# Eight full expert tiles ahead of the last routing, a hand-made TensorE order, and logits with moving tokens: attention and a routed expert layer on one core

## The chip, the cores and the metric

The kernel runs on one core of a Trainium2 chip. The metric is the device time of one execution in microseconds (us); lower is better. A core has TensorE (matmul), VectorE, ScalarE, GpSimd (POOL in the profile), SyncE (SP, here the engine that issues the large transfers) and 16 DMA engines that all queues share. All data are float32, apart from the masks.

## The reference

Attention with a window of 32 (heads 0 to 3: the last 32 positions; heads 4 to 7: every fourth of the last 128), then a layer of eight experts with one expert to a token. A token takes the expert with the largest logit, unless its local gate is at least 0.5: then it keeps the expert of the token before it.

```python
# q, k, v: (8, 8, 576, 64); x: (8, 576, 512); w_gate (512, 8); w1 (8, 512, 1024); w2 (8, 1024, 512)
scores = np.where(masks, scale * q @ k.T, -1e9)
x = softmax(scores) @ v                         # heads side by side: 512 features
logits = einsum('bsd,de->bse', x, w_gate)
local_gate = sigmoid(x @ w_local)
for b in range(B):
    prev_e = -1
    for s in range(S):
        fresh_e = argmax(logits[b, s])
        e = fresh_e if s == 0 or local_gate[b, s] < 0.5 else prev_e
        prev_e = e
        p = softmax(logits[b, s])
        h = np.maximum(x[b, s] @ w1[e], 0.0)
        out[b, s] = p[e] * (h @ w2[e])
```

## The kernel before, in words

Two stages follow each other. The attention stage loops over 32 pairs of heads, four pairs (NP = 4) to a batch. `load(n)` puts three transfers for pair n on SP's queue (`kt`, `qt`, `vt`; 1.27 MB together, three buffers each). `scores(n)` makes twelve matmul instructions into three PSUM tiles `sc` (six products; a float32 product is two instructions); VectorE adds the mask (line 232) and ScalarE takes the exponential (235). `values(n)` multiplies by `vt` into `pv` (278), and VectorE divides by the row sums (280 to 282) into `x`.

After the four pairs of a batch comes its routing, which the dictionary `steps` spreads over the following iterations. `store` writes `x` to `xd` in DRAM. `x_turn` transposes `x` into `xt` (306). `logits` uses blocks of 96 tokens of `xt` as the stationary operand and moves the nine columns of `wg`: 24 products, 48 instructions a batch (320). `carry` turns each token's code (its fresh expert and its position) into one row of 576 and runs a maximum along it (357), which carries the last fresh expert on. `choose` turns the row back and makes the one-hot `oh`, the running counts `cum` and the pair `pay` (token, gate), whose first column (390) needs nothing but a constant and a free buffer. `place(b)` works out each token's slot in the table `tab` in DRAM, and POOL writes `pay` there by six indirect transfers (411), a scatter for each block of 96 tokens. All write to `tab`, so each waits until the one before has landed.

When all batches are placed, the counts give the list of tiles: an expert's tokens are cut into tiles of 128, at most NT = 43 tiles. POOL reads the tiles' rows of `tab` into `tr` (471), which two transposes turn into `tok` and `gate` (476, 477).

The expert stage loops over 43 tiles. `gather` fetches 128 rows of `xd` (501), `features` transposes them (509, 511), `hidden` makes 64 instructions of 128 columns (519) and two Relu passes (522), `output` 16 instructions of 512 columns (528), VectorE's product with the gate (530) and an indirect write to `out` (531). `weights` reads the tile's expert number on SP and reloads `w1s` and `w2s` (two buffers each, 2 MB a load), unless the buffer holds that expert already. Both pairs of buffers are filled with expert 0 at the very start, behind `load(2)` on SP's queue.

A planner sets the order of instructions on each engine: it runs the program with its own durations, and an instruction goes when its operands and a buffer are free there. So an instruction late in the text can be moved far ahead. On the chip each engine keeps that order and waits where an operand is late. A second version of the whole, for inputs out of range, follows in a branch that isn't taken here.

Of the kernel before, what the change touches and what calls it, by code (L numbers as in the profile page):

```python
# [10 lines left out]
F32 = mybir.dt.float32  # L11
# [25 lines left out]
UB = 2  # L37
NU = NB // UB
VW = DH + 1
MASK = -1e30  # L40
# [13 lines left out]

FRESH = -(2.0 ** -23)

# [3 lines left out]
C_IDX = C_TRI + QB  # L60
# [3 lines left out]
C_TOK = C_CODE + NB  # L64
C_ROW = C_TOK + NB
# [4 lines left out]
def constants():  # L70

    c = np.zeros((P, C_ALL), np.float32)
    c[:, C_ID:C_TRI] = np.eye(P)
    c[:QB, C_TRI:C_IDX] = np.triu(np.ones((QB, QB)), 1)
    c[:, C_IDX:C_REV] = np.arange(E)
    c[:, C_REV:C_BASE] = E - np.arange(E)
    c[:, C_BASE:C_CODE] = np.arange(E) * CAP * P
    s = np.arange(NB)[None] * QB + np.arange(P)[:, None]
    c[:, C_CODE:C_TOK] = s * E + E
    c[:, C_TOK:C_ROW] = s  # L80
    c[:, C_ROW:C_COL] = np.arange(NT)
    c[:, C_COL] = np.arange(P)
    return c
# [29 lines left out]
def dilated_attn_locality_moe_kernel(  # L113
# [16 lines left out]
    wg = keep.tile([P, DK, E + 1], F32, name="wg")  # L130
# [14 lines left out]
def whole(ctx, tc, exact, bad, q, k, v, wgl, w1, w2, con, msk, qmk, out, cst, wg, ones):  # L145
    nc = tc.nc
    name = "exact" if exact else "plain"
    keep = ctx.enter_context(tc.tile_pool(name=f"keep_{name}", bufs=1))
    dram = ctx.enter_context(tc.tile_pool(name=f"dram_{name}", bufs=1, space=DRAM))

    xd = dram.tile([N + 1, D], F32, name="xd")
    tab = dram.tile([(PADS + 1) * P, 2], F32, name="tab")

    tok = keep.tile([P, NT], I32, name="tok")
    gate = keep.tile([P, NT], F32, name="gate")
    experts = keep.tile([1, NT], I32, name="experts")
    ident = cst[:, C_ID:C_TRI]
    w1s = [keep.tile([P, FK, DK, P], F32, name=f"w1s{i}") for i in range(2)]
    w2s = [keep.tile([P, FK, D], F32, name=f"w2s{i}") for i in range(2)]

    with ExitStack() as attn:
        def pool(name, bufs, **kw):
            return attn.enter_context(tc.tile_pool(name=name, bufs=bufs, **kw))

        once = pool("once", 1)
        ins = pool("ins", 3)
        work = pool("work", 2 if exact else 6)
        xp = pool("xp", 2)
        sm = pool("sm", 3)
        scp = pool("scp", 1 if exact else 3, space=PSUM)  # L170
        pvp = pool("pvp", 1, space=PSUM)
        msp = pool("msp", 2, space=PSUM)
        if exact:
            ptp = pool("ptp", 1, space=PSUM)

        mk = once.tile([KW, 2 * NB * QB], BF16, name="mk")
        rec = once.tile([QB, B * NP, 2, NB], F32, name="rec")
        loaded = {}

        def load(n):  # L180
            qt = ins.tile([P, NB, 2, QB], F32, name="qt")
            kt = ins.tile([P, WIN + S], F32, name="kt")
            vt = ins.tile([P, 2, NB, VW], F32, name="vt")
            nc.sync.dma_start(out=kt, in_=k[n])
            nc.sync.dma_start(out=qt.rearrange("p i u s -> p (i u s)"), in_=q[n])
            nc.sync.dma_start(out=vt.rearrange("p u i e -> p (u i e)"), in_=v[n])
            loaded[n] = kt, qt, vt

        load(0)
        if not exact:  # L190
            nc.sync.dma_start(out=mk, in_=msk)
        else:
            qm = once.tile([QB, QB + 2 * NB * KW], BF16, name="qm")
            nc.sync.dma_start(out=qm, in_=qmk)
        load(1)
        if not exact:
            nc.sync.dma_start(out=cst, in_=con)
            nc.sync.dma_start(out=wg.rearrange("p k e -> p (k e)"), in_=wgl)
        load(2)


        fill = once.tile([P, PADS + 1, 2], F32, name="fill")
        nc.vector.memset(fill[:, :, 0], NOBODY)
        nc.vector.memset(fill[:, :, 1], 0.0)
        nc.gpsimd.dma_start(out=tab.rearrange("(p r) c -> p (r c)", p=P), in_=fill.rearrange("p r c -> p (r c)"))
        zero = once.tile([1, D], F32, name="zero")
        nc.vector.memset(zero, 0.0)
        nc.gpsimd.dma_start(out=xd[N:N + 1], in_=zero)
        before = once.tile([QB, E], F32, name="before")
        nc.vector.memset(before, 0.0)  # L210
# [5 lines left out]
        xs, prob, routes = {}, {}, {}  # L216

        def scores(n):

            kt, qt, _ = loaded[n]  # L220
            kind = (n % NP) // (NP // 2)
            prob[n] = []
            for c in range(NU):
                sc = scp.tile([KW, 2, UB, QB], F32, name="sc")
                for i in range(UB):
                    s = (c * UB + i) * QB
                    nc.tensor.matmul(sc[:, :, i], lhsT=kt[:, s:s + KW], rhs=qt[:, c * UB + i],  # L227
                                     start=True, stop=True)
                pr = work.tile([KW, 2, UB, QB], F32, name="pr")
                at = (kind * NB + c * UB) * QB  # L230
                flat = pr.rearrange("w u i p -> w u (i p)")
                nc.vector.scalar_tensor_tensor(  # L232
                    flat, sc.rearrange("w u i p -> w u (i p)"), CEIL,
                    mk[:, at:at + UB * QB].unsqueeze(1).to_broadcast([KW, 2, UB * QB]), Alu.min, Alu.add)
                nc.scalar.activation(pr, pr, Act.Exp, scale=SCALE)  # L235
                prob[n].append(pr)

        def scores_exact(n):

            kt, qt, _ = loaded[n]  # L240
            kind = (n % NP) // (NP // 2)
            prob[n] = []
            for c in range(NU):
                sc = scp.tile([QB, UB, 2, KW], F32, name="sc")
                first = True
                for i in range(UB):
                    s = (c * UB + i) * QB
                    at = QB + (kind * NB + c * UB + i) * KW
                    for u in range(2):
                        nc.tensor.matmul(sc[:, i, u], lhsT=qm[:, :QB], rhs=qm[:, at:at + KW],  # L250
                                         start=first, stop=False, skip_group_check=True)
                        nc.tensor.matmul(sc[:, i, u], lhsT=qt[:, c * UB + i, u], rhs=kt[:, s:s + KW],
                                         start=False, stop=True, skip_group_check=True)
                        first = False
                top = sm.tile([QB, UB, 2], F32, name="top")
                nc.vector.tensor_reduce(top, sc, axis=AX.X, op=Alu.max, negate=True)
                nc.vector.tensor_scalar_mul(top, top, SCALE)
                ex = work.tile([QB, UB, 2, KW], F32, name="exq")
                pt = ptp.tile([KW, 2, UB, QB], F32, name="pt")
                for i in range(UB):  # L260
                    for u in range(2):
                        nc.scalar.activation(ex[:, i, u], sc[:, i, u], Act.Exp, scale=SCALE, bias=top[:, i, u:u + 1])
                        nc.tensor.transpose(pt[:, u, i], ex[:, i, u], ident[:QB, :QB])
                pr = work.tile([KW, 2, UB, QB], F32, name="pr", bufs=6)
                nc.vector.tensor_copy(pr, pt)
                prob[n].append(pr)

        def values(n):
            b, g = divmod(n, NP)
            vt = loaded.pop(n)[2]  # L270
            ps = prob.pop(n)
            if g == 0:
                xs[b] = xp.tile([QB, NB, D], F32, name="x")
            pv = pvp.tile([QB, 2, 512], F32, name="pv")
            pv = pv[:, :, :NB * VW].rearrange("p u (i e) -> p u i e", i=NB)
            for i in range(NB):
                for u in range(2):
                    nc.tensor.matmul(pv[:, u, i], lhsT=ps[i // UB][:, u, i % UB], rhs=vt[:, u, i],  # L278
                                     start=True, stop=True)
            nc.vector.tensor_scalar(rec[:, n], pv[:, :, :, DH], FLOOR, None, Alu.max)  # L280
            nc.vector.reciprocal(rec[:, n], rec[:, n])
            nc.vector.tensor_tensor(  # L282
                xs[b][:, :, g * P:(g + 1) * P].rearrange("p i (u d) -> p u i d", u=2), pv[:, :, :, :DH],
                rec[:, n].unsqueeze(3).to_broadcast([QB, 2, NB, DH]), op=Alu.mult)

        def store(b):

            x = xs[b]
            to = xd[b * S:(b + 1) * S]
            half = D // 2  # L290
            nc.sync.dma_start(out=to[:, :half].rearrange("(i p) f -> p i f", p=QB), in_=x[:, :, :half])
            to = to.rearrange("(j g o) f -> j g o f", g=2, o=2)
# [310 lines left out]
```

## Time and profile before

| | before |
|---|---|
| times of three runs | 1024.3, 1025.12, 1027.89 us; median 1025.12 us |
| profiled execution | 1014.79 us, its span 1013.0 us |
| TensorE busy | 897.6 us of the span, mean granted clock 0.903 |
| VectorE, ScalarE, POOL busy | 209.1, 128.3, 132.5 us |
| DMA | 140.71 MB moved, mean 139 GB/s |
| indirect writes to `tab` | 48, busy 44.7 us on POOL, idle before them 306.6 us |

The span is the time from the first to the last instruction of one execution. The page cuts it into 40 equal slices, here of 25.3 us, and gives each engine's busy share in tenths: attention fills the first 13 slices, the transition the 14th and part of the 15th, the expert tiles the rest. A table of stretches gives for each stretch its length, the busy time and count of instructions of TensorE's matmuls and weight loads, VectorE, ScalarE and POOL, then the granted TensorE clock, the DMA engines' busy share and GB/s. In a list of instructions the bracket at the end is the idle time of the engine before the row and what ended it; in a list of waits the numbers are microseconds in total, times, and sometimes the longest.

### The profile page before, as it was taken

The numbers are of one execution on the slowest core, as the hardware profiler recorded it, in microseconds if no ns is written. First come the engines' busy times: TensorE is split into PE (matmuls) and PEld (weight loads), VectorE is DVE, ScalarE is ACT, GpSimd is POOL, SyncE is SP. The second block draws the span as 40 slices with busy tenths as digits, with TensorE's granted clock in tenths as the row PEclk, the third lists the DMA queues.
The fourth block names the chain that finished last, engine by engine and source line by source line (L and its number), as shares of the span: only waits on it lengthen the run. The fifth ranks groups of instructions, "written<-read, shape, count | busy, mean of one in ns | idle before, by whom it ended". The sixth has DMA issues, their size and how long they took to land.

```text
span 1013.0 us, 13463 instructions
## 1 busy us (share of the span) xinstructions
PE 897.6 (89%) x5522; PEld 711.1 (70%) x5522; DVE 209.1 (21%) x583; ACT 128.3 (13%) x255; POOL 132.5 (13%) x141
## 2 busy tenths in 40 slices
PE   6599859697698149999999999999999999999996
PEld 6598859687697146677677767766776776677674
DVE  3364434444354200010101011010101101010100
ACT  2222303123032000000000000000000000000000
POOL 0002111110111221110101111010111111011100
PEclk9787967677686569999999999999999999999998
DMA  9976837566450010370461073450181281730000
GB/s 376 372 263 166 210 83 199 117 154 188 100 139 24 1 55 32 115 284 28 144 259 42 32 280 127 181 223 22 61 323 45 93 307 43 280 122 32 21 10 4
DMA packets 37512, 140.71 MB, mean 139 GB/s; under 512 B 6451, under 2 KB 15795, under 8 KB 33344
## 3 DMA queue, kind: packets, MB, share of 16 engines
q1 hardware_dynamic: 28720, 118.64, 35.9%
q0 software_dynamic: 8720, 21.10, 6.2%
q8 instruction: 46, 0.75, 0.3%
q14 instruction: 26, 0.21, 0.1%
HBM read 242.14 MB, written 21.04 MB: 260 GB/s over the span
## 4 chain that ended last, share of the span: by engine, by line
PE 71%; DMA 20%; issue 3%; ACT 2%; DVE 2%; SPq 0%; POOL 0%; POOLq 0%; ACTq 0%; DVEq 0%
PE hp L519 30%; PE yp L528 30%; DMA tab<-pay,pi 16%; PE pv L278 4%; PE sc L227 3%; DMA qt<-in_q_dram 2%; PE lp L320 2%; ACT h L522 2%; DMA cst<-in_con_dram 1%; PE tp L306 1%; DMA tr<-tab,ri 0%; PE cp L363 0%; ACT pr L235 0%; DVE pr L232 0%; DMA xg<-xd,tok 0%
## 5 line engine op out<-in xcount | busy, mean ns | idle before, releaser
L519 PEld LDWEIGHTS hp<-xgt,w1s 128*128 128x128 f32 x2752 | 315.4, 193 | 20.1 <-issue 20.1
L519 PE MATMUL hp<-xgt,w1s 128*128 128x128 f32 x2752 | 315.6, 276 | 0.0
L528 PE MATMUL yp<-w2s,h 128*128 128x512 f32 x688 | 306.8, 599 | 3.7 <-ACT h L522 1.3
L528 PEld LDWEIGHTS yp<-w2s,h 128*128 128x128 f32 x688 | 127.2, 190 | 155.2 <-issue 144.6
L278 PE MATMUL pv<-vt,pr 128*96 128x65 f32 x768 | 93.9, 286 | 41.5 <-ACT pr L235 38.5
L522 ACT ACTIVATE h<-hp 128x512 f32<-128x512 f32 x86 | 46.7, 595 | 625.8 <-PE hp L519 572.9
L278 PEld LDWEIGHTS pv<-vt,pr 128*96 128x96 f32 x768 | 89.4, 201 | 45.5 <-ACT pr L235 41.8
L530 DVE TENSOR_SCALAR y<-yp,gate 128x512 f32<-128x512 f32 x43 | 32.3, 751 | 399.9 <-PE yp L528 399.9
L227 PE MATMUL sc<-qt,kt 128*128 128x192 f32 x384 | 86.8, 387 | 15.1 <-DMA qt<-in_q_dram 15.0
L531 POOL DMA_INDIRECT out_dram<-y,tok x43 | 42.8, 994 | 415.7 <-DVE y L530 408.0
L227 PEld LDWEIGHTS sc<-qt,kt 128*128 128x128 f32 x384 | 80.0, 237 | 15.6 <-issue 15.3
L411 POOL DMA_INDIRECT tab<-pay,pi x48 | 44.7, 932 | 306.6 <-DMA tab<-pay,pi 154.2
L235 ACT ACTIVATE pr<-pr 128x384 f32<-128x384 f32 x96 | 48.8, 522 | 171.4 <-DVE pr L232 165.8
L511 DVE COPY xgt<-tp 128x512 f32<-128x512 f32 x43 | 28.5, 688 | 181.5 <-PE tp L509 181.5
L501 POOL DMA_INDIRECT xg<-xd,tok x43 | 42.0, 978 | 146.9 <-PE tp L509 136.7
L232 DVE SCALAR_TENSOR_TENSOR pr<-sc,mk 128x384 f32<-128x384 f32 x96 | 51.9, 552 | 44.9 <-PE sc L227 35.0
L320 PE MATMUL lp<-wg,xt 128*96 128x9 f32 x384 | 48.9, 268 | 0.5
L320 PEld LDWEIGHTS lp<-wg,xt 128*96 128x96 f32 x384 | 47.6, 220 | 2.4 <-ACT xt L311 1.7
L306 PE MATMUL tp<-cst,x 96*128 96x96 f32 x192 | 29.6, 269 | 8.5 <-ACT xt L309 4.0
L282 DVE TENSOR_TENSOR x<-pv,rec 96x768 f32<-96x768 f32 x32 | 30.5, 953 | 1.0
L306 PEld LDWEIGHTS tp<-cst,x 96*128 96x128 f32 x192 | 20.7, 154 | 13.4 <-ACT xt L309 8.2
L509 PE MATMUL tp<-cst,xg 128*128 128x128 f32 x172 | 24.7, 280 | 4.6 <-DMA xg<-xd,tok 4.6
(83 smaller groups left out, 187.6 us busy)
## 6 DMA issues: line engine op xcount, KB each, us to landing
w1s<-in_w_dram SPq DMA_DIRECT2D x45, 2048.0 KB
w2s<-in_w_dram SPq DMA_DIRECT2D x45, 2048.0 KB
qt<-in_q_dram SPq DMA_DIRECT2D x32, 576.0 KB
vt<-in_v_dram SPq DMA_DIRECT2D x32, 390.0 KB
kt<-in_k_dram SPq DMA_DIRECT2D x32, 304.0 KB
xd<-x SPq DMA_DIRECT2D x8, 576.0 KB
xd<-x SPq DMA_DIRECT2D x16, 192.0 KB
xd<-x SPq DMA_DIRECT2D x16, 96.0 KB
```

The costliest lines, as they stand in the source:

```text
L227: nc.tensor.matmul(sc[:, :, i], lhsT=kt[:, s:s + KW], rhs=qt[:, c * UB + i], start=True, stop=True)
L232: nc.vector.scalar_tensor_tensor(flat, sc.rearrange("w u i p -> w u (i p)"), CEIL, mk[:, at:at + UB * QB].unsqueeze(1).to_broadcast([KW, 2 ...
L235: nc.scalar.activation(pr, pr, Act.Exp, scale=SCALE)
L278: nc.tensor.matmul(pv[:, u, i], lhsT=ps[i // UB][:, u, i % UB], rhs=vt[:, u, i], start=True, stop=True)
L306: nc.tensor.transpose(tp[:, i * QB:(i + 1) * QB], x[:, j * HB + i, kk * P:(kk + 1) * P], ident[:QB, :QB])
L320: nc.tensor.matmul(lp[:, i], lhsT=st["xt"][:, kk, i * QB:(i + 1) * QB], rhs=wg[:, kk], start=(kk == 0), stop=(kk == DK - 1))
L411: nc.gpsimd.indirect_dma_start(out=tab, out_offset=bass.IndirectOffsetOnAxis(ap=pi[:, i:i + 1], axis=0), in_=st["pay"][:, i], in_offset=None)
L501: nc.gpsimd.indirect_dma_start(out=x, out_offset=None, in_=xd, in_offset=bass.IndirectOffsetOnAxis(ap=tok[:, t:t + 1], axis=0))
L519: nc.tensor.matmul(hp[:, m], lhsT=w1s[t % 2][:, m, kk], rhs=x[:, kk], start=(kk == 0), stop=(kk == DK - 1))
L522: nc.scalar.activation(h[:, m:m + FK // 2], hp[:, m:m + FK // 2], Act.Relu)
L528: nc.tensor.matmul(yp, lhsT=h[:, m], rhs=w2s[t % 2][:, m], start=(m == 0), stop=(m == FK - 1))
L531: nc.gpsimd.indirect_dma_start(out=out, out_offset=bass.IndirectOffsetOnAxis(ap=tok[:, t:t + 1], axis=0), in_=y, in_offset=None, bounds_ch ...
```

## The change

It has these parts.

1. *Early tiles.* Once five batches (EARLY) are routed, `table(False)` works out from their counts which tiles are full already, and takes the first eight (FIRST) of them. They are gathered and computed first; `done` notes how many each expert has used, and `table(True)` lists the other 35. `gather` of an early tile reads only the first five batches of `xd`.
2. *Routing in small steps.* The nine steps of a batch's routing (ten where a table follows) stand in a list `waiting`, and `gap()` takes one of them: after the scores, after each half of the values, and in the expert stage after each half of `hidden` and after `output`. So the last batch's routing lies between the matmuls of tiles 0 to 3. `tokens(True)` stands ahead of tile 5.
3. *TensorE's order by hand.* `tc.manual_schedule(engines={ET.PE})`: TensorE's instructions go in the order of the text. The other engines stay with the planner.
4. *Logits.* `wg`, padded to 32 columns, is now stationary and the tokens move: four groups of 144 tokens, each into its own 32 columns of the array, 16 products a batch. ScalarE copies the result out and two transposes bring the tokens back to partitions.
5. *Blocks of 72.* Routing works in eight blocks of 72 tokens instead of six of 96, so `place` makes eight scatters. The maximum runs along eight rows at once, with a second small run over their ends (`carry_over`, `carry_in`).
6. *Buffers and loads.* One pool of six PSUM banks serves everything but `pv`; `sm` has two buffers instead of three; `load(2)` moves into the loop, and the first weights (`load_first`) go behind `load(14)`. In the expert stage the load of `w1` for tile t + 2 is issued after `hidden(t)`, that of `w2` after `output(t)`. The check of `rec` stands after the last tile.

```diff
+TB = 72
+NJ = S // TB
+NC = 4
+LW = 32
+EARLY, FIRST = 5, 8
...
+    ctx.enter_context(tc.manual_schedule(engines={ET.PE}))
-        sm = pool("sm", 3)
-        scp = pool("scp", 1 if exact else 3, space=PSUM)
-        msp = pool("msp", 2, space=PSUM)
+    sm = pool("sm", 2)
+    banks = pool("banks", 6, space=PSUM)
     pvp = pool("pvp", 1, space=PSUM)
...
-        load(2)
-        for i in range(2):
-            nc.sync.dma_start(out=w1s[i]..., in_=w1[0])
-            nc.sync.dma_start(out=w2s[i]..., in_=w2[0])
+    def load_first():            # the same four transfers
...
     def logits(b):
-            for i in range(NB):
-                for kk in range(DK):
-                    nc.tensor.matmul(lp[:, i], lhsT=st["xt"][:, kk, i * QB:(i + 1) * QB], rhs=wg[:, kk], ...)
+        for kk in range(DK):
+            for c in range(NC):
+                nc.tensor.matmul(lp[c * LW:(c + 1) * LW], lhsT=wg[:, kk],
+                                 rhs=st["xt"][:, kk, c * (S // NC):(c + 1) * (S // NC)],
+                                 start=(kk == 0), stop=(kk == DK - 1), skip_group_check=True,
+                                 tile_position=(0, c * LW))
+        nc.scalar.copy(le, lp)
...
+    def carry_over(b):
+        nc.tensor.transpose(lp, st["run"][:, TB - 1:TB], ident[:NJ, :NJ])
+        nc.vector.tensor_copy(ends[:, 1:], lp[:, :NJ - 1])
+        nc.vector.tensor_tensor_scan(over, ends, ends, 0.0, Alu.max, Alu.max)
+    def carry_in(b):
+        nc.tensor.matmul(op, lhsT=st["over"], rhs=ones[0:1, 0:1], start=True, stop=True)
+        nc.vector.tensor_scalar(st["run"], st["run"], op, None, Alu.max)
...
     def place(b):
-            for i in range(NB):
+        for j in range(NJ):
             nc.gpsimd.indirect_dma_start(out=tab, ..., in_=st["pay"][:, j], in_offset=None)
...
+    def table(late):
+        nt = NT - FIRST if late else FIRST
+        nc.tensor.matmul(cn, lhsT=ones[:TB], rhs=routes[B - 1 if late else EARLY - 1]["cum"][:, NJ], ...)
+        nc.vector.tensor_scalar(ni, cn, float(P - 1) if late else 0.0, None, Alu.add)
+        if late:
+            nc.vector.tensor_tensor(nf, nf, tiles["done"], op=Alu.subtract)
...
+    def route(b):
+        waiting.extend([lambda: (store(b), x_turn(b, 0), x_turn(b, 1)), lambda: (x_turn(b, 2), x_turn(b, 3)),
+                        lambda: logits(b), lambda: fresh(b), lambda: carry(b), lambda: carry_over(b),
+                        lambda: carry_in(b), lambda: choose(b), lambda: place(b)])
+        if b == EARLY - 1:
+            waiting.append(lambda: table(False))
+        if b == B - 1:
+            waiting.append(lambda: table(True))
+
+    for n in range(B * NP + 1):
+        if n < B * NP:
+            (scores_exact if exact else scores)(n)
+        gap()
+        if n:
+            values(n - 1, 0)
+            gap()
+            values(n - 1, 1)
+            gap()
+            if n % NP == 0:
+                route(n // NP - 1)
+        if n + 2 < B * NP:
+            load(n + 2)
+        if n == 3 * NP:
+            load_first()
+        if n == B * NP - 2:
+            tokens(False)
+            for t in range(3):
+                gather(t)
+            for t in range(2):
+                weights(t, False)
+                weights(t, True)
+
+    features(0)
+    for t in range(NT):
+        if t == FIRST - 3:
+            tokens(True)
+        hidden(t, 0)
+        gap()
+        hidden(t, 1)
+        gap()
+        if t + 2 < NT:
+            weights(t + 2, False)
+        if t + 1 < NT:
+            features(t + 1)
+        if t + 3 < NT:
+            gather(t + 3)
+        output(t)
+        gap()
+        if t + 2 < NT:
+            weights(t + 2, True)
```

More of the change, by code (lines that the diff above doesn't have):

```diff
@@ L238, in scores_exact @@
[L238 to L266, printed above, removed]
@@ L469, in whole @@
+        ri = new([nt, 1], "ri", I32)
         nc.vector.tensor_scalar(ri, at, float(PADS), None, Alu.min)
[L470 removed]
+        tiles["rows", late] = tr = new([nt, P, 2], "tr")
         nc.gpsimd.indirect_dma_start(
@@ new lines, in tokens, with of_tile @@
+    def tokens(late):
+        tr = tiles["rows", late]
+        nt = NT - FIRST if late else FIRST
+        for c, (what, dtype) in enumerate((("tok", I32), ("gate", F32))):
+            tp = bank([P, nt], "tt")
+            nc.tensor.transpose(tp, tr[:, :, c], ident[:nt, :nt])
+            tiles[what, late] = to = once.tile([P, nt], dtype, name=f"{what}{late:d}")
+            nc.vector.tensor_copy(to, tp)
+    def of_tile(what, t):
+        late = t >= FIRST
+        t -= FIRST * late
+        return tiles[what, late][0:1 if what == "experts" else P, t:t + 1]
```

630 lines of the change are left out of this document (323 added, 307 removed).

## The prediction

> **What bounds the kernel now.** I read the page's engine and slice rows, then the chain in order of time, then a table of stretches, and last the waits around the table `tab`, since the chain names it.
>
> ```profile
> span 1013.0 us, 13463 instructions
> PE 897.6 (89%) x5522; PEld 711.1 (70%) x5522; DVE 209.1 (21%) x583; ACT 128.3 (13%) x255; POOL 132.5 (13%) x141
> PE   6599859697698149999999999999999999999996
> ...
> 13.39 24.72 DMA qt<-in_q_dram
> ...
> 357.93 4.70 DMA tr<-tab,ri
> ...
> 369.95 9.35 PE hp L519 x72
> ...
> 997.67 7.15 PE yp L528 x16
> ...
> 145.00:190.00 45.00, 35.28 (x238) 33.76 (x238) 17.91 (x59) 9.96 (x21) 5.98 (x6) 0.69 0.62 142
> ...
> 329.60:369.00 39.40, 5.30 (x27) 4.50 (x28) 5.53 (x35) 0.00 (x0) 11.77 (x13) 0.50 0.07 17
> ...
> 400.00:1000.00 600.00, 596.29 (x3429) 434.67 (x3428) 57.20 (x81) 44.53 (x82) 77.04 (x78) 1.00 0.36 130
> ```
>
> There are three stages. From 370 us on, 43 expert tiles keep TensorE full (596.3 of 600 us busy, clock 1.00): 369.95 to 997.67 + 7.15 = 1004.8 is 634.9 us, **14.76 us a tile**, and 1013.0 - 1004.8 = 8.2 us of tail. Between 329.6 and 369 TensorE works 5.3 of 39.4 us: the routing of the last batch, its scatters, the read `tr`, and the first gathers. Before that, attention leaves TensorE idle a fifth of the time and its clock at about 0.7.
>
> What holds attention is in the waits of POOL and VectorE:
>
> ```profile
> POOL tab L411 <- DMA tab<-pay,pi: 154.2, 40, 6.8
> ...
> DVE pay L390: 39.5, 5
> ...
> 75.58 0.98 POOL L411 DMA_INDIRECT tab<-pay,pi  x1 [72.36 <-DVE pi L409]
> ...
> 113.48 0.91 POOL L411 DMA_INDIRECT tab<-pay,pi  x1 [12.60 <-DVE pi L409]
> ...
> 141.23 0.91 POOL L411 DMA_INDIRECT tab<-pay,pi  x1 [4.89 <-DMA tab<-pay,pi]
> 156.89 0.91 POOL L411 DMA_INDIRECT tab<-pay,pi  x1 [14.76 <-DVE pi L409]
> ...
> 284.28 0.91 POOL L411 DMA_INDIRECT tab<-pay,pi  x1 [11.34 <-DVE pi L409]
> ...
> 306.35 0.91 POOL L411 DMA_INDIRECT tab<-pay,pi  x1 [2.17 <-DMA tab<-pay,pi]
> 315.32 0.91 POOL L411 DMA_INDIRECT tab<-pay,pi  x1 [8.06 <-DVE pi L409]
> ...
> 332.99 0.91 POOL L411 DMA_INDIRECT tab<-pay,pi  x1 [1.73 <-DMA tab<-pay,pi]
> 337.40 0.91 POOL L411 DMA_INDIRECT tab<-pay,pi  x1 [3.50 <-DVE gc L463]
> ...
> 353.67 0.91 POOL L411 DMA_INDIRECT tab<-pay,pi  x1 [2.87 <-DMA tab<-pay,pi]
> ...
> 146.33 0.17 DVE L390 TENSOR_SCALAR pay<-cst 96x6 f32<-96x6 f32 x1 [10.41 <-DMA tab<-pay,pi]
> ```
>
> Each batch places its tokens by six scatters into `tab`, and each waits until the one before has landed. Start to start that is (141.23 - 113.48)/5 = 5.55 us in batch 1, (306.35 - 284.28)/5 = 4.41 in batch 5, 3.53 in batch 6 and 3.25 in batch 7, where nearly nothing else moves. Over all 40 waits it is 154.2/40 = 3.86 plus the 0.93 of a scatter (44.7/48 on the page) = 4.79, so 5.24 over the 30 of batches 0 to 5. The chain reaches the other engines through `pay`: three buffers, so VectorE's write for batch b + 3 waits for batch b's last scatter, and it stands ahead of the masking of scores. At 146.33 VectorE had stood for 10.41 us. The period (156.89 - 113.48 = 43.4 us) is 33 us of scatters and 10.5 us from the released `pay` to the next first scatter. So scatters set the pace of attention, not TensorE.
>
> **The change, part by part.** I follow one chain: place(0), five periods P, place(5), place(6), the start M of the tiles, the late table, then 38 tiles that nothing can hurry.
>
> *Start.* The 8.4 MB of first weights leave the head of SP's queue, where load 3 stood behind them:
>
> ```profile
> 5.33 4.18 PE L227 MATMUL sc<-qt,kt 128*128 128x192 f32 x12 [5.33 <-DMA qt<-in_q_dram]
> ...
> 38.25 3.77 PE L227 MATMUL sc<-qt,kt 128*128 128x192 f32 x12 [9.64 <-DMA qt<-in_q_dram]
> ...
> 13.40:38.30 24.90, 11.25 (x106) 10.68 (x104) 7.03 (x17) 5.70 (x12) 0.00 (x0) 0.86 1.01 421
> ```
>
> The scores of pair 3 began at 38.25. Loads 0 to 3 with masks and constants are 6 MB, 14 us at the 421 GB/s of that stretch; TensorE itself needs three iterations of some 5.5 us after 5.33, so pair 3 begins at about 22. From 38.25 to place(0) at 75.58 were seven iterations, 5.33 us each. Now place(0) ends iteration 7, five after pair 3; with 5.6 each place(0) is at **50** (44 to 60). The weights come behind load 14 instead: 8.4 MB at 421 GB/s are 20 us, and pair 15 waits up to 13 of them. I cost it at nothing, because P has that much slack over TensorE's work (below); without the slack it is 13 us.
>
> *Scatters: 8 of 72 rows instead of 6 of 96, and two `pay` buffers instead of three.* The new row count is not in the trace. Upper bound of one: 5.24, if rows don't matter. Lower bound: the 0.93 of issue kept and the other 4.31 scaled by 72/96, 4.2. I take the middle, L = **4.7**, since the quiet 3.25 of batch 7 shows that a good part depends on neither rows nor load. Eight are 37.6 us a batch against 31.4 before. `pay` of batch b + 2 now waits for batch b. TensorE alone has its order by hand; VectorE's is still planned, and six scatters put that write three iterations behind place(b), so eight put it about four behind, close to place(b + 1). What follows the wait before the next place, 10.5 us before, I take as d = **2** (bounds 0 and 10.5; nearest are the positions just counted). P = 8L + d = 37.6 + 2 = **39.6 us**, not much under the 43.4 of before.
>
> The Trainium skill's page "DMA: Bandwidth & Descriptors", section "Why a DMA increments its semaphore by 16 and not by 1", speaks against the smaller scatter: a transfer uses the largest number of engines up to 16 that divides its rows, so 96 rows go to 16 engines and 72 to 12, six rows on each in both. By it L would stay at 5.24, P be 43.9 and the sum below 5 x 4.3 = 22 us longer; no run here shows 72 rows.
>
> *TensorE's own work per batch.* It must fit into P:
>
> ```profile
> 288.23 2.15 PE L227 MATMUL sc<-qt,kt 128*128 128x192 f32 x12
> ...
> 290.21 2.17 PE L278 MATMUL pv<-vt,pr 128*96 128x65 f32 x24
> ...
> 293.84 5.04 PE L320 MATMUL lp<-wg,xt 128*96 128x9 f32 x48
> ...
> 316.79 7.85 PE L320 MATMUL lp<-wg,xt 128*96 128x9 f32 x48
> L306 PE MATMUL tp<-cst,x 96*128 96x96 f32 x192 | 29.6, 269 | 8.5 <-ACT xt L309 4.0
> ```
>
> Four pairs are 4 x (2.15 + 2.17) = 17.3, the turns 29.6/8 = 3.7. Logits become 16 products, 32 instructions of 144 columns in place of 48: at 2.15/12 x 144/192 = 0.134 us each 4.3 us if the four column groups follow each other, 1.1 if they overlap, against 5.04 to 7.85. Small transposes 1.5, and in hand order TensorE stands in some seven gaps for VectorE or ScalarE, about 1 us each. That is 31 to 34 us, below 39.6. So the logits, the hand order, the row-wise scan and the longer VectorE work (some ten more operations of 0.15 to 0.2 us) are worth nothing while the scatters set the pace; without that cover logits give 1 to 7 us a batch, the gaps cost 7.
>
> *To the first tile.* place(5) = 50 + 5 x 39.6 = 248. The early table's read of `tab` follows batch 4's last scatter and lands about 5 us later (4.70 for `tr`); its tokens are wanted in iteration 30, two to three later, so hidden. Its gathers stand on POOL among batch 5's scatters. Batch 5's eight take L' = 4.2 (loads run out; 4.41 before): 33.6, + 2, place(6) = 283.6. TensorE's four iterations, 26 us, lie beside it. The last values and the first turn: 6. **M = 290**, 80 us before the 369.95 of now.
>
> *Tiles beside the last routing.* Routing 7 puts about 6 us of matmuls into three tiles; place(7) = 290 + 3 x 14.76 + 6 = 340. Its scatters at L'' = 3.5 (3.25 quiet, 4.41 loaded), 28 us, with 3 us of gathers and output scatters that POOL runs between, and 5.5 for `tr` and the turn: tokens at 376.5. Tile 5 is due at 290 + 5 x 14.76 + 6 = 370 and waits 7. POOL does the tiles' gathers and output scatters in between:
>
> ```profile
> DMA to landing us min/median/max: 3.3/4.3/8.5
> ...
> DMA to landing us min/median/max: 2.1/2.8/9.7
> ```
>
> These are landings of gathers and of output scatters; three gathers are ahead and `y` has two buffers, so a delay of 8 us there is hidden; more is paid in full. Storing batch 7 is behind the weights of tiles 0 and 1 on SP, but nobody reads it before tile 8.
>
> *Weights.* From the reference's routing the early tiles are of experts 0,0,0,1,1,1,2,2 and the late ones begin with 0 again: 20 tiles need other weights than two tiles before, 14 now; ten of them are tiles 3, 4 and 6 to 13. 4.2 MB in 14.76 us are 284 GB/s, under the 421 shown, and 22 us lie between issue and use: nothing. At 200 GB/s it would be 6 us on each of eight tiles, 48.
>
> *The rest.* Tiles have the same matmuls; the page shows no TensorE wait to take away there. The check of `rec` moves behind the last tile: one matmul beside the 8.2 us tail.
>
> **Sum.** 377 + 38 x 14.76 (561) + 8.2 = **946 us** of span against 1013.0. The profiled execution took 1014.79, 1.8 above its span, and the median shown is 1025.12, 10.3 above that; with both kept, **958 us**.
>
> **The rivals.** Each is the same sum with other L, L', L'' and d.
>
> *The scatters let go.* Rows count in full (4.2) and d = 0: P = 33.6, place(5) = 218, L' = 3.7, place(6) = 248, M = 254, place(7) = 304, tokens at 337 with L'' = 3.1; 906, median **918**. If TensorE's 31 us were the pace, place(5) = 205 and 26 + 6 us on M = 237; place(7) = 287, tokens at 320 and the end at 889, median 901. For it: the quiet scatters at 3.25. Against: shorter attention loads the DMA queues more (0.62 busy at 145 to 190 us).
>
> *Rows don't matter and the plan fits worse.* L = 5.24, d = 5: P = 47, place(5) = 285, L' = 4.9, place(6) = 329, M = 335, place(7) = 385, L'' = 4.2 and 8.5 give 427: 996, median **1008**. For it: 5.55 in batch 1 at that load.
>
> *Slower: VectorE's `pay` stays one iteration ahead of place.* Then d = 10.5 as before and P = 8 x 5.24 + 10.5 = 52.4, place(5) = 312, place(6) = 312 + 39 + 10.5 = 362, M = 368, place(7) = 418, tokens at 460: 1029, median **1041**. It decides from P = 49 on, where the end reaches 1013. For it: all five periods before had that d. Against: eight scatters move the planned end by a third.
>
> **How the numbers follow.** Chances: forecast 0.45, scatters let go 0.25, rows don't matter 0.20, slower 0.10. The range goes from the second case's lower part, 905, to just past the third, 1012; outside lie the fourth and the fastest part of the second. 0.3% (3 us) is about what a measurement of this kernel tells from no change: faster 0.88, same 0.03, slower 0.09.
>
> **What would show it.** Scatters eight to a batch, 4.2 to 5.2 us apart, with `pay` still waiting for `tab`; place(0) near 50, scores of pair 3 near 22; a TensorE wait for `qt` near pair 15; tile 0 near 290, tile 5 waiting for `tr`; 14.8 us a tile after it; no stretch like 329.6 to 369. Wrong would make it: scatters no longer waited for, a plan that puts gathers behind all scatters of batch 6 on POOL, or tiles 3 to 13 waiting for weights.

## The result, and the profile after

Before 1024.83 us (median; 1024.3 to 1027.89), after **978.52 us** (974.91 to 981.2): a ratio of 0.954, 95% interval 0.9504 to 0.9576. The forecast was 958 within 905 to 1012. The way lies as forecast, the place where it ends doesn't: the late tokens came 41 us after their forecast, the tiles gave 10 of that back, 2 went to a longer tail, and the 12 us that the forecast added for the median over the profile's span weren't needed this time. The last is luck: without it the forecast would have been off by 33 us and not by 20.

The page of the changed kernel: span, engines, TensorE in 40 slices of 24.5 us, and two groups (busy us, mean ns; then the engine's idle time ahead of them and what ended it).

```profile
span 979.0 us, 13125 instructions
...
PE 817.4 (84%) x5310; PEld 641.2 (65%) x5310; DVE 202.0 (21%) x639; ACT 131.3 (13%) x263; POOL 148.3 (15%) x158
...
PE   6981728283562999599999999999999999999995
...
L447 POOL DMA_INDIRECT tab<-pay,pi x64 | 59.8, 934 | 308.1 <-DMA tab<-pay,pi 221.0
...
L426 DVE TENSOR_SCALAR pay<-cst 72x8 f32<-72x8 f32 x8 | 1.2, 166 | 110.6 <-DMA tab<-pay,pi 110.6
```

TensorE is full from the 14th slice on (but for the 17th). The first tile begins at 324.98 us where it began at 369.95, 45 us sooner. But attention is emptier: slices 7 to 13 are 8, 2, 8, 3, 5, 6, 2 where 9, 6, 9, 7, 6, 9, 8 stood. `pay` waits 110.6 us where it waited 39.5.

POOL's rows, a batch's first scatter and a few others (start, duration, and in the bracket how long POOL had stood and for what):

```profile
53.45 0.99 POOL L447 DMA_INDIRECT tab<-pay,pi  x1 [50.22 <-DVE pi L445]
...
100.07 0.93 POOL L447 DMA_INDIRECT tab<-pay,pi  x1 [5.68 <-DVE pi L445]
...
275.05 0.92 POOL L447 DMA_INDIRECT tab<-pay,pi  x1 [3.34 <-DMA tab<-pay,pi]
...
281.35 0.96 POOL L447 DMA_INDIRECT tab<-pay,pi  x1 [2.08 <-DMA tr_early<-tab,ri_early]
...
377.51 0.96 POOL L447 DMA_INDIRECT tab<-pay,pi  x1 [0.31 <-issue]
...
412.62 0.92 POOL L447 DMA_INDIRECT tab<-pay,pi  x1 [6.02 <-DMA tab<-pay,pi]
415.26 0.95 POOL L508 DMA_INDIRECT tr_late<-tab,ri_late  x1 [1.72 <-DMA tab<-pay,pi]
```

The period is (281.35 - 53.45)/5 = 45.6 us. Between the start of batch 4's last scatter (275.05) and that of batch 5's first lie 6.3 us.

The chain of the changed kernel in order of time (start, duration) shows such a handover, here that to batch 2, and further on the first tile and two whole tiles:

```profile
141.57 3.05 DMA tab<-pay,pi
...
144.87 1.39 DVE pr L241 x3
...
153.61 4.52 DMA tab<-pay,pi
...
324.98 5.89 PE hp L557 x32
...
607.87 7.14 PE hp L557 x64
615.45 6.87 PE yp L565 x16
622.32 7.14 PE hp L557 x64
```

The last scatter of batch 1 lands at 144.62, VectorE writes `pay`, and only then go the masked scores that it had kept waiting, products on TensorE, the choosing and `pi`: 9.0 us of other engines' work between two scatters. This is the longest of the five handovers. Ahead of batches 1, 3 and 4 the write of `pay` stands later in VectorE's order, behind most of the choosing, and from the landing to the next scatter (195.54 for batch 3) are 3.2 us. VectorE stands for `pay` each time, and TensorE with it, except that TensorE's wait ahead of batch 2 was first one of 17.9 us for queries and only then 7.0 us for VectorE. VectorE and TensorE ahead of batch 3, then of batch 2:

```profile
192.40 0.17 DVE L426 TENSOR_SCALAR pay<-cst 72x8 f32<-72x8 f32 x1 [15.74 <-DMA tab<-pay,pi]
192.69 0.50 PE L437 MATMUL kp<-cum,ones 72*72 72x64 f32 x2 [17.60 <-DVE cum L415]
...
134.06 4.18 PE L236 MATMUL sc<-qt,kt 128*128 128x192 f32 x12 [17.88 <-DMA qt<-in_q_dram]
...
144.70 0.17 DVE L426 TENSOR_SCALAR pay<-cst 72x8 f32<-72x8 f32 x1 [27.18 <-DMA tab<-pay,pi]
```

### The profile page after: what moved, and what is told of

Its sections match the earlier page's. It is cut to its first block, busy times and chain, and to the rows that moved or that the text cites. A ratio compares the mean times of both kernels' runs of the same rounds, so it can differ in the third digit from the quotient of the medians.

```text
span 979.0 us, 13125 instructions
## 1 busy us (share of the span) xinstructions
PE 817.4 (84%) x5310; PEld 641.2 (65%) x5310; DVE 202.0 (21%) x639; ACT 131.3 (13%) x263; POOL 148.3 (15%) x158
## 4 chain that ended last, share of the span: by engine, by line
PE 66%; DMA 26%; issue 4%; DVE 2%; POOL 1%; SPq 0%; POOLq 0%; DVEq 0%
PE hp L557 30%; PE yp L565 29%; DMA tab<-pay,pi 25%; PE sc L236 2%; PE pv L287 2%; PE tp L546 2%; DMA qt<-in_q_dram 1%; POOL tab L447 1%; DVE pr L241 0%; PE tp L317 0%; POOL xg L539 0%; PE kp L437 0%; DVE x L292 0%; DMA tr_late<-tab,ri_late 0%; PE lp L332 0%
## 5 line engine op out<-in xcount | busy, mean ns | idle before, releaser
L557 PE MATMUL hp<-xgt,w1s 128*128 128x128 f32 x2752 | 319.1, 277 | 1.2 <-DVE xgt L548 1.2
L565 PE MATMUL yp<-w2s,h 128*128 128x512 f32 x688 | 302.4, 592 | 0.0
L559 ACT ACTIVATE h<-hp 128x512 f32<-128x512 f32 x86 | 51.4, 597 | 599.4 <-PE hp L557 599.4
L236 PE MATMUL sc<-qt,kt 128*128 128x192 f32 x384 | 86.5, 386 | 25.5 <-DMA qt<-in_q_dram 25.5
L447 POOL DMA_INDIRECT tab<-pay,pi x64 | 59.8, 934 | 308.1 <-DMA tab<-pay,pi 221.0
L236 PEld LDWEIGHTS sc<-qt,kt 128*128 128x128 f32 x384 | 77.2, 229 | 27.7 <-issue 27.6
L437 PE MATMUL kp<-cum,ones 72*72 72x64 f32 x16 | 3.6, 326 | 96.2 <-DVE cum L415 96.2
L287 PE MATMUL pv<-vt,pr 128*96 128x65 f32 x768 | 78.2, 256 | 0.0
L287 PEld LDWEIGHTS pv<-vt,pr 128*96 128x96 f32 x768 | 74.8, 173 | 0.4
L437 PEld LDWEIGHTS kp<-cum,ones 72*72 72x72 f32 x16 | 2.3, 199 | 97.2 <-DVE cum L415 97.2
L426 DVE TENSOR_SCALAR pay<-cst 72x8 f32<-72x8 f32 x8 | 1.2, 166 | 110.6 <-DMA tab<-pay,pi 110.6
L546 PEld LDWEIGHTS tp<-cst,xg 128*128 128x128 f32 x172 | 20.4, 143 | 0.0
```

What stands on the lines that cost most here:

```text
L447: nc.gpsimd.indirect_dma_start(out=tab, out_offset=bass.IndirectOffsetOnAxis(ap=pi[:, j:j + 1], axis=0), in_=st["pay"][:, j], in_offset=None)
L546: nc.tensor.transpose(tp[:, kk], x[:, kk * P:(kk + 1) * P], ident)
L557: nc.tensor.matmul(hp[:, m], lhsT=w1s[t % 2][:, half * FK // 2 + m, kk], rhs=x[:, kk], start=(kk == 0), stop=(kk == DK - 1))
L559: nc.scalar.activation(ht[t][:, half * FK // 2:(half + 1) * FK // 2], hp, Act.Relu)
L565: nc.tensor.matmul(yp, lhsT=h[:, m], rhs=w2s[t % 2][:, m], start=(m == 0), stop=(m == FK - 1))
```

## The experiments

The first four ask what holds attention, the next three why, three more which part of the change is worth what, and the last two what is left. Spans are given where places in the trace are compared. Each set of runs timed the kernel before again (medians 1024.83, 1028.85, 1028.95 and 1027.49 us), so times of different sets are comparable to about 4 us, and ratios more closely.

**1. Eight buffers for `pay` and `pi`.** All else stays.

```diff
-        st["pay"] = pay = sm.tile([TB, NJ, 2], F32, name="pay")
+        st["pay"] = pay = sm.tile([TB, NJ, 2], F32, name="pay", bufs=B)
-        pi = sm.tile([TB, NJ], I32, name="pi")
+        pi = sm.tile([TB, NJ], I32, name="pi", bufs=B)
```

> The changed kernel with eight buffers for pay and pi instead of two, so that VectorE never waits for a scatter. Theory S (the chain of scatters into one table, each waiting for the landing of the one before, sets the pace up to tile 5; VectorE's wait is only how TensorE feels it): the 64 scatters close up, the few us between a batch's last landing and the next first scatter go, attention ends earlier, but TensorE then waits for the early and the late table instead; the late tokens come at about 400 instead of 418 and the span falls from 979 to about 960 (950 to 972). Rival V (the wait for the buffer, 110.6 us of idle VectorE, is itself the cost): the wait goes and TensorE's 25 us of work a batch become the pace, span about 850 to 870. Rival T (TensorE with its hand order and gaps is the pace): 979.

963.22 us, ratio 0.9344 (0.9284 to 0.9404). The wait of `pay` is gone, but the scatters are a lock of their own. The waits, and TensorE's row at the early table:

```profile
POOL tab L447 <- DMA tab<-pay,pi: 227.5, 56, 9.7
...
271.75 0.37 PE L517 MATMUL tt<-cst,tr_early 8*128 8x8 f32 x2 [55.83 <-DMA tr_early<-tab,ri_early]
```

Every scatter but the eight that follow something else now waits for the one before. Attention runs ahead of them, and TensorE then stands for 55.83 us until the early table is there.

**2. Two tables.** Even and odd scatters write to tables of their own, so two can be under way; the rows are read from both and put together by minimum and maximum.

```diff
-                out=tab, out_offset=...
+                out=tabs[j % len(tabs)], out_offset=...
```

> The changed kernel with two tables in DRAM: even blocks scatter into one, odd blocks into the other, and the tiles' rows are read from both and merged on VectorE (minimum of the tokens, maximum of the gates). Two scatters can be in flight. Theory S: a batch's chain is four landings of some 5.6 us, 22 us, about TensorE's own 25 to 27; place(5) near 190 instead of 281, tile 0 near 220 instead of 325, late tokens near 306, span about 867 (850 to 900). Theory T (TensorE is the pace): 979. Theory D (the DMA engines' total work is the pace, and scatters only queue behind it): landings get longer as attention gets shorter, two in flight take 10 us each, and the span stays above 950.

961.24 us, 0.9342 (0.9294 to 0.9391): far from 867. Waits, and POOL's last scatter of batch 3 and first of batch 4:

```profile
DVE pay L427 <- DMA tab<-pay,pi: 88.9, 6, 23.3
...
208.75 0.92 POOL L448 DMA_INDIRECT tab<-pay,pi  x1 [0.70 <-DMA tab<-pay,pi]
228.27 0.93 POOL L448 DMA_INDIRECT tab<-pay,pi  x1 [18.61 <-DVE pi L446]
```

The eight scatters of batch 3 take 21 us from first start to last start (from 187.89) instead of 36, and the handover grows from 6.5 to 19.5 us. Faster scatters alone are paid back at the wait of `pay`: the planner puts the write further ahead, and from its release (212.48) to the next scatter lie 15.8 us of masks, carry and choosing, where it was 3.1 in the changed kernel (192.40 to 195.54).

**3. Both.**

> The changed kernel with both: two tables in DRAM and eight buffers for pay and pi. Each alone gave about 17 us. Theory S+ (two locks in series: the chain into one table holds POOL, and VectorE's write of pay, which the planner puts where it believes the scatters to be done, holds VectorE until they really are; taking one away leaves the other): now both are gone, TensorE's 25 to 28 us a batch are the pace, tile 0 near 222 to 235, no wait ahead of tile 5 beyond some 10 us, span about 880 (865 to 905). Theory D (the DMA engines' work is the pace): two scatters in flight take twice as long, span 935 to 960. Additive (two independent savings): about 943.

915.13 us, 0.8891 (0.8857 to 0.8926). Cure 1 took 15 us from the changed kernel, cure 2 took 17, both together 63 (by the ratios 2.0, 2.0 and 6.5% of the kernel before): two locks in series, either of which holds what the other lets go. The time lies above the expected 865 to 905; the longest waits that are left are these:

```profile
PE sc L237 <- DMA qt<-in_q_dram: 34.5, 4, 23.2
DVE tr_late L516 <- DMA part_late<-tab,ri_late: 22.6, 1, 22.6
DVE tr_early L516 <- DMA part_early<-tab,ri_early: 19.3, 1, 19.3
```

**4. Six scatters of 96 rows** in the changed kernel: `TB = 96` and three column groups for the logits (`NC = 3`).

> The changed kernel with six blocks of 96 tokens instead of eight of 72 (three column groups of 192 tokens in the logits), so six scatters a batch. Theory S with landings that do not depend on rows: 6 x 5.4 + 3 = 36 us a batch instead of 45.6; place(5) near 231, tile 0 near 267, late tokens near 357, span about 918 (905 to 935). Rival R (a scatter's time goes with its rows, so 6 x 96 cost what 8 x 72 cost): 979, with 7.2 us from scatter to scatter. Theory T: 979.

961.93 us, 0.935 (0.9303 to 0.9398). The expected 918 took 5.4 us for a scatter and 3 for a handover; the five batches' means are 5.67, 6.97, 6.02, 5.91 and 6.43 us (6.2 together), the period is 43.1 = 6 x 6.2 + 5.9, and the wait of `pay` stays (95.0 us). The times from issue to landing of before's scatters (96 rows), of the changed kernel's (72) and of this one's (96), one row each:

```profile
DMA to landing us min/median/max: 2.5/4.3/6.6
```

```profile
DMA to landing us min/median/max: 2.0/4.0/8.0
```

```profile
DMA to landing us min/median/max: 2.1/5.1/9.4
```

**5. Logits five times over** (`for kk in list(range(DK)) * 5`): about 5 us more of TensorE in each batch, in a stage where TensorE stands idle for 19 to 28 us of each period. Each repetition starts its sums anew, so the logits stay what they were.

> The changed kernel with every logits product computed five times (160 instructions a batch instead of 32, about 5 us more of TensorE; the result is overwritten and unchanged). Chain only (a batch lasts as long as its eight landings, TensorE has 17 us or more to spare): attention unchanged, only the last batch's logits among the tiles count, span about 984 (979 to 990). Planner's place (a batch lasts as long as its real landings plus the work that the plan puts behind the write of pay): half or all of the 5 us is seen in each of six batches, span 995 to 1015. TensorE as the pace: 1015 or more.

1019.79 us, 0.9896 (0.9856 to 0.9935). The span is 1019.4 us, 40.4 above the changed kernel's, and the five periods are 50.7 us in the mean instead of 45.6. So idle TensorE time wasn't free time. But it isn't the extra products themselves that hold the scatters up. VectorE's `pay` ahead of batch 1, that batch's first scatter, the logits of batch 2 beside its scatters, TensorE's wait after them, and the first scatter of batch 2:

```profile
99.54 0.17 DVE L426 TENSOR_SCALAR pay<-cst 72x8 f32<-72x8 f32 x1 [20.27 <-DMA tab<-pay,pi]
...
110.05 0.92 POOL L447 DMA_INDIRECT tab<-pay,pi  x1 [13.01 <-DVE pi L445]
...
118.94 5.14 PE L332 MATMUL lp<-xt,wg 128*32 128x144 f32 x160
...
154.25 2.15 PE L287 MATMUL pv<-vt,pr 128*96 128x65 f32 x12 [12.85 <-DVE ends L386]
...
163.47 0.93 POOL L447 DMA_INDIRECT tab<-pay,pi  x1 [13.05 <-DVE pi L445]
```

```profile
DVE pay L426 <- DMA tab<-pay,pi: 92.6, 5, 22.8
```

`pay` still waits for the scatters in five batches, and TensorE still stands behind it, so TensorE hasn't become the pace. What has grown is the handover: ahead of batches 1 to 4 POOL stands 12.8 to 13.6 us for `pi`, where it stood 5.6 in three and 11.1 in one. From the release of `pay` (99.54) to the next scatter lie 10.5 us instead of the changed kernel's 3.1 (96.93 to 100.07). In VectorE's order the write now stands ahead of the masks, the carry and the choosing, not behind most of them. That the planner moved it because it counts the longer products is the likely reason, and wasn't tried alone.

**6. Three buffers** for `pay` and `pi` instead of two (`bufs=3`).

> The changed kernel with three buffers for pay and pi in place of two; everything else as it is. Theory 'planner's place': what VectorE stands behind is the place at which the planner put the write of pay in its queue (among the next batch's choosing), and three buffers leave that place as it is from the fourth batch on; but the DMA that a write waits for is then a batch older and long landed, so the waits of pay go only if age alone decides. The planner, which knows of three buffers, can put the write a batch earlier again, and in its order the writes of batches 3 to 7 stand where they stood: then the wait stays and the time is 979 us (970 to 985). Rival 'two buffers are too few': one more buffer takes the wait away, and the time is that with eight, 961 us (955 to 967).

979.15 us, 0.952 (0.9464 to 0.9576): nothing.

```profile
DVE pay L426 <- DMA tab<-pay,pi: 100.0, 5, 27.4
```

The planner writes `pay` as soon as it believes a buffer free. With a third buffer it writes for one batch further on, at the same places and behind the same scatters: three writes at 14.70 us, the next at 95.78 and 143.92 after waits of 21.8 and 27.4, where there were two at 15.20 and the next at 96.93 and 144.70 after 20.1 and 27.2.

**7. Two buffers, and a `pay` that can't be written early.** Its first column is made from the batch's own `ef` (times nought), so it can't stand ahead of its own batch's choosing.

```diff
-        nc.vector.tensor_scalar(pay[:, :, 0], cst[:TB, C_TOK:C_ROW], float(b * S), None, Alu.add)
+        nc.vector.scalar_tensor_tensor(pay[:, :, 0], ef, 0.0, cst[:TB, C_TOK:C_ROW], Alu.mult, Alu.add)
+        nc.vector.tensor_scalar(pay[:, :, 0], pay[:, :, 0], float(b * S), None, Alu.add)
```

> The changed kernel with its two buffers for pay and pi, but pay's first column is computed from the batch's own ef (times nought), so that the write can't stand in VectorE's queue ahead of the choosing of its own batch; it costs one more small VectorE instruction a batch. Theory 'planner's place': VectorE's wait of 110.6 us for the scatters goes nearly altogether, the scatters of a batch start 2 to 8 us after the last of the batch before, the five periods are about 8 x 5.43 = 43.4 us in place of 45.6, more under the load of the weights, and the time is 961 to 971 us, about that with eight buffers (963). Rival 'two buffers are too few': the wait for the buffer stays wherever the write stands, and the time is 979 us (972 to 985).

963.75 us, 0.9379 (0.9324 to 0.9434): the time that eight buffers give, with two.

```profile
DVE pay L426 <- DMA tab<-pay,pi: 39.0, 3, 14.3
```

So it isn't the number of buffers but where the write stands. The wait went to 39.0 us, not to nothing as expected; and the first period became 60.5 us (attention runs on beside the weights' burst: from 75 to 100 us the DMA engines are wholly busy with 356 GB/s, against 0.49 and 148 GB/s there in the changed kernel), the next three 43.7 = 8 x 5.46 us. Place(5) came at 275.97, only 5 us sooner than in the changed kernel; the other 13 of the 18.5 us by which `tr_late` came sooner (396.74) lie in batches 5 to 7, whose attention had run ahead of the scatters.

**8. No early tiles** (`FIRST = 0`, one table of 43 tiles after all routing).

> The changed kernel without its first part: one table after all eight batches, all 43 tiles after it; the last batch's routing runs alone. Theory S: attention ends at the same 323; the last routing, eight scatters and the first gathers then stand alone as before, first tile near 390, span about 1023 (1010 to 1040), slower than before the change: the rest of the change would cost more than it brings, and the early tiles alone carry the gain. Rival (the early tiles are hidden anyway, since tile 5 waits for the same chain): 985.

1020.28 us, 0.9913 (0.9886 to 0.9939). TensorE's turn of the table (read from 374.79 on) with the 41.68 us that it had stood for it, and the first tile:

```profile
379.97 0.46 PE L508 MATMUL tt<-cst,tr_late 43*128 43x43 f32 x2 [41.68 <-DMA tr_late<-tab,ri_late]
...
385.99 9.18 PE L548 MATMUL hp<-xgt,w1s 128*128 128x128 f32 x64 [0.78 <-DVE xgt L539]
```

By the ratios (0.9913 against 0.954) the early tiles carry some four fifths of the change's gain. The first tile begins at 324.98 instead of 385.99, and of these 61 us 13.3 go back at the wait for the late table and some 7 in the routing between the first tiles.

**9. No hand order** (the line `manual_schedule` left out).

> The changed kernel without the hand order: the planner orders TensorE as well. Theory S+: the scatters and pay hold attention just the same. Tiles take about 14.76 us again instead of 14.48, 43 x 0.28 = 12 us: span about 991 (980 to 1005). Rival (the hand order is what brings attention forward, or what costs there through TensorE's waits in the gaps): below 970 or above 1010.

990.18 us, 0.9617 (0.9583 to 0.9651). The number was right, the reason wrong: the tiles are as fast under the planner (chain in order of time), so the loss (11.7 us of time, 8.8 of span) comes from attention, where the period is 48.6 us instead of 45.6 and the late table is read 8 us later (423.34).

```profile
602.39 7.14 PE hp L556 x64
616.84 7.14 PE hp L556 x64
```

**10. The kernel before with eight buffers** for `pay` and `pi`, and nothing else.

> The kernel before the change, with eight buffers for pay and pi and nothing else. Theory S+: VectorE's 39.5 us of waits go; six landings of 5.3 us, 32 us, are about TensorE's own work there, so attention ends about 40 us earlier, the last routing and the 43 tiles stay: span about 970 (960 to 985), as much as the whole change brought. Rival (TensorE's order, the start and the early tiles are what was missing): 1005 to 1015.

982.93 us, 0.9549 (0.9515 to 0.9583). Two words in the old kernel bring what the whole change brings. Its waits, in which `pay` no longer occurs:

```profile
POOL tab L411 <- DMA tab<-pay,pi: 177.1, 44, 7.5
```

**11. and 12. What was left.** From experiment 3: rows put together after TensorE's transposes, so that VectorE doesn't stand for them; twelve early tiles instead of eight; and the first weights as four loads, one each behind loads 14, 18, 22 and 26 (in 12 with blocks of 96 and six scatters).

```diff
-EARLY, FIRST = 5, 8
+EARLY, FIRST = 5, 12
...
-        if n == 3 * NP:
-            load_first()
+        if n % NP == 0 and 0 <= n // NP - 3 < 4:
+            load_first(n // NP - 3)        # one 2 MB load each
```

> Eight buffers for pay and pi, two tables (even and odd scatters) whose rows are put together after TensorE's transposes, so that VectorE no longer stands for the rows to be read back (19.3 and 22.6 us in the run with both cures); the first weights as four loads of 2 MB, one after each of loads 14, 18, 22 and 26, in place of 8 MB at once (TensorE stood 34.5 us for queries there); and twelve tiles ahead of the last routing in place of eight. From 915 us: less at most 34.5 for the queries, less the share of 41.9 us of VectorE's wait that TensorE felt. Theory 'the waits seen there are what is left': 875 us (860 to 895). Rival 'the 16 DMA engines are the bound in attention': first expert product not before 262 us, as there, and the time stays within 905 to 915.

> The same as the kernel with all of these cures, but routed 96 rows at a time in six scatters a batch in place of 72 rows in eight. Spacing of scatters measured so far: 6.2 us at 96 rows against 5.43 us at 72, so 37 us a batch against 43. If the scatters are still the lock: some 5 x 6 = 30 us less than the kernel with eight. If attention's own work and loads are: within 8 us of it. With the cures the scatters no longer stand in one chain, so the second is expected: 0 to 8 us apart, either way.

886.94 us, 0.8637 (0.858 to 0.8694), and 881.92 us, 0.8574 (0.852 to 0.8628); the two can't be told apart. The first tile begins at 246.8 and 244.3 us. The scatters no longer set the pace, since six or eight of them make no difference; the DMA engines are now the busiest part of attention. The stretch from 50 to 250 us, once of the changed kernel and once of experiment 11, with the DMA share and GB/s at the end:

```profile
50.00:250.00 200.00, 109.07 (x979) 103.39 (x980) 75.44 (x293) 45.86 (x103) 31.71 (x35) 0.75 0.65 190
```

```profile
50.00:250.00 200.00, 147.25 (x1317) 138.88 (x1318) 107.25 (x408) 59.55 (x132) 53.82 (x58) 0.86 0.89 234
```

and the chain of experiment 11 in order of time, where the long pieces are now loads (91 of the 137 us from 62.7 to 199.8). That loads are now what bounds attention is read from this chain and wasn't tried:

```profile
111.35 13.71 DMA w2s<-in_w_dram
125.08 9.59 DMA qt<-in_q_dram
...
142.31 15.40 DMA w1s<-in_w_dram
```

## Why the prediction was right, and where its sum was off

The direction and the mechanism held: eight scatters in a chain set attention's pace, `pay` waits for them, the early tiles fill the last routing, and nothing can hurry the last 38 tiles. By its own steps:

| step | forecast | measured | off by |
|---|---|---|---|
| place(0) | 50 | 53.45 | +3.4 |
| five periods P | 198 | 227.9 | +29.9 |
| place(5) to first tile M | 42 | 43.6 | +1.6 |
| M to place(7) | 50 | 52.5 | +2.5 |
| place(7) to late tokens | 36.5 | 40.4 | +3.9 |
| 38 tiles | 561 | 550.7 | -10.3 |
| tail | 8.2 | 10.4 | +2.2 |

Their sum is +33 us of span; the median that was forecast 12 above the span lies 0.5 below it.

- **The term that was mis-sized is L**, one scatter of 72 rows: forecast 4.7 us, measured 5.43 (five batches' means 5.72, 5.93, 5.06, 5.19, 5.24). Eight times 0.73 over five batches is 29 of the 29.9 us. The handover d was right as a mean (45.58 - 8 x 5.43 = 2.1; forecast 2), though it is made of four of about 1 us and one of 6.6, so the third case, with L = 5.24 and d = 5, had the better L and the worse d.
- I took the middle of 4.2 and 5.24, as if a quarter fewer rows had to save something. The Trainium skill's page "DMA: Bandwidth & Descriptors" (section "Why a DMA increments its semaphore by 16 and not by 1") spoke for the other answer: by its rule for the number of engines, 72 rows on 12 and 96 on 16 are six rows on each. With L kept at 5.24 the forecast would have been 980. From before to after the traces agree with that (5.24 to 5.43 us at a DMA share of 0.66 and 0.65 between 50 and 250 us), but experiment 4 doesn't: 96 rows in the new kernel took 6.2 us, at a share of 0.72. Nearly alone, 72 rows take 2.96 us (batch 7 of experiment 8) and 96 took 3.25. What of the 0.8 us is rows and what is load stays open.
- **"Worth nothing while the scatters set the pace" was wrong** for TensorE's work: in experiment 5 about 5 us more of it made the periods 5.1 us longer. The step that failed compared work and period as totals, 31 to 34 us against 39.6 (measured: 23 to 26 us busy in a period of 45.6). What counts is how much of the routing stands behind the released `pay`, for that part is in the chain, and in experiment 5 it grew from 3.1 to 10.5 us ahead of batch 1, although the products had room. So what shorter logits brought in this change stays open. They do take less: 32 instructions in 1.21 us, where one after the other would be 4.0 (twelve score products of 192 columns take 2.01 us in the same chain).

```profile
35.73 1.21 PE lp L332 x32
```

- **The weights' burst**, costed at nothing: TensorE waits 25.5 us for `qt`, 17.9 of it in one place, the scatters beside it were the slowest, 5.93 us, and the handover behind it was the longest. Whether it cost time in this kernel wasn't tried alone; in experiment 3, where the scatters no longer covered it, it was among the largest waits.

```profile
PE sc L236 <- DMA qt<-in_q_dram: 25.5, 3, 17.9
...
PE tt L517 <- DMA tr_late<-tab,ri_late: 13.3, 1, 13.3
```

- **Tile 5** waited 13.3 us for the late table (forecast 7), since the last scatters were 5.0 us apart and not 3.5.
- **A tile takes 14.45 us, not 14.76.** I wrote that there is no TensorE wait to take away. There was one, in the kernel before, between the last `hp` and the first `yp`. The waits of its weight loads, and its chain:

```profile
PEld yp L528 <- ACT h L522: 9.9, 27, 0.9
...
621.27 7.16 PE hp L519 x64
628.51 0.61 ACT h L522
```

In the changed kernel that wait is gone: `hidden` comes in two halves, the first Relu runs beside the second half's products, only the next tile's transposes lie between, and `yp` starts at 615.45, 0.44 us after `hp`. Experiment 9 shows that this holds without the hand order too.
- **The rival "slower"** named the right danger, `pay` as the place where the two orders meet, with d = 10.5; here d was 2.1. Experiment 6 shows that a third buffer wouldn't have moved it.

## What to carry to other kernels

Where an engine's order is fixed from planned durations, a small write to a reused buffer is placed where the plan believes a transfer to have ended; if transfers are really longer, the whole engine stands there, and everything between it and the next transfer, on other engines too, is added to the transfers' chain. Work that seems to fit into idle time can move that write and so cost its full length (experiment 5). Look for a tiny instruction with a long wait, and try more buffers (as many as there are uses: one more did nothing) or a dependence that keeps it late, before rebuilding a stage. With two locks in series each cure alone looks small (15 and 17 us); try them together (63 us) before dropping either.

## What the runs showed of the hardware

Indirect writes of less than a KB (72 rows of 8 bytes) cost 3.0 us each in a chain when little else moves (DMA share 0.01, batch 7 of experiment 8), and 5.1 to 5.9 us in the five periods of the changed kernel, at shares of 0.54 to 0.73. At the end of the weights' burst one took 11.2 us (98.64 to 109.81 in experiment 7, with the DMA engines wholly busy). Here what ran beside them mattered more than the step from 72 to 96 rows, which was 0.3 us when little else moved. Four column groups of 32 let TensorE run 32 float32 instructions of 144 columns in 1.21 us, 3.3 times faster than one after another at the rate of the same chain's score products.
